# Transposes of the logits ahead of the third stage's first product, in the odd steps of a long convolution with soft mixture of experts

## The chip, the cores and the metric

The program runs on one core of a Trainium2 chip. The metric is the device time of one execution in microseconds (us). Engines: PE (TensorE, with its weight loads as PEld), DVE (VectorE), ACT (ScalarE), POOL (GpSimd) and SP (SyncE, which here only issues transfers). Each engine works through its own instructions in the order of the program and waits on semaphores for the others. All data are float32.

## What is computed

A causal convolution of 8 sequences (5696 tokens, 128 channels) with a filter as long as the sequence, done by Fourier transforms; then a mixture of experts with soft slots over all 45568 tokens. The reference, cut to that:

```python
def _attn_ref(x, h):                       # x (8, 5696, 128), h (5696, 128)
    Xf = np.fft.rfft(x, n=2*S, axis=1)
    Hf = np.fft.rfft(h, n=2*S, axis=0)
    return np.fft.irfft(Xf * Hf[None], n=2*S, axis=1)[:, :S, :]

def _moe_ref(x, phi, w1, w2):              # x (45568, 128), 8 experts of 4 slots
    logits = x @ phi                       # (45568, 32)
    d = softmax(logits, axis=0)            # over the tokens
    slot_input = (d.T @ x).reshape(E, S_per_e, D)
    slot_out[e] = relu(slot_input[e] @ w1[e]) @ w2[e]
    c = softmax(logits, axis=1)            # over the slots
    return c @ slot_out
```

## The kernel before

The transform of a sequence is split into two lengths, 90 and 64, and done as matrix products in three stages. Between stages the data go through HBM, since the next stage needs another axis on the partitions.

- *First stage* (`first_low`, `first_high`, L217): a chunk of the input, `xc`, is folded into sums and differences `x` (`fold`, L207, on POOL once the second stage runs), multiplied by `s1`, copied by ACT from PSUM into `fst` (L220), and stored to `f`.
- *Second stage*: `stage_b1` (L263) multiplies a loaded unit `gt` by `wt` into PSUM `bt`; DVE multiplies that with the filter's spectrum (L281 twice, L290 twice) into `yf`. `stage_b2` (L305) multiplies `yf` by `vt`; ACT copies into `zst` (L311), which is stored to `z`. A step's last unit is left in `wait_b2`, and its L305 is issued in the next step's turn, behind the L263 of the next unit.
- *Third stage*, per pair of chunks T: `load_pair` (L342, five transfers, about 1.3 MB) brings `zc`, of which there is one buffer; `stage_c1` (L361) makes the tokens `y`. It is a generator in three parts: first half (two products `b_`, `a_`; ACT copies `b_` into `y`, L370; DVE adds and subtracts `a_`, L366 and L367), second half (two more products; ACT copies into `om`, L374; the generator yields ahead of the rest), and the rest (`after`: L366 and L367 again, and four operations of POOL, L380).
- *Slots*: `stage_c2` (L391) transposes `y` into `yt`; `stage_c3` (L400) forms the logits, copied by ACT to `lt` (L403); `column_max` (L411 to L419, DVE) keeps the running extreme `low` over tokens. `stage_c4` transposes `lt` on PE (L429, four instructions), copies it to `L` (L433, ACT), writes the exponentials `dt` (L435, ACT, with `low` as bias) and `dn` (L440, ACT), clears a corner of `dt` (L437, POOL), takes a row maximum `rm` of `L` (L444, DVE) and subtracts it (L445, POOL). `stage_c5` (L452) transposes `dt`, `softmax` (L460 to L466) finishes the weights over slots, `dispatch` (L478) sums tokens into slots, `stage_c6` (L504) transposes the weights into `cbatch`.

**Order.** The schedule is manual: every engine works in the order in which the Python code issues. The main loop runs over steps t = 0 to 80. A step processes one chunk of the first stage, one or two units of the second, and half a pair's work of the third; a pair thus takes two steps, a sequence eight (in one step of the eight a unit is half as large). The order within a step is a string, one letter per piece of work: `ORDER_E` for odd t, `ORDER_O` for even t, and the `FILL_` strings for t below 9. In `ORDER_E`:

- `x` loads input, `X` and `Y` are the first stage (products, copies, stores), `f` folds the next input,
- `1`, `j`, `w` take the three parts of `stage_c1` of pair T = (t - 27)/2,
- `4` is `stage_c4` of the pair before (lag of two steps), `b` a turn of the second stage, `5` is `stage_c5`, `s` is `softmax`.

In `ORDER_O`: `z` is `load_pair`, `P` loads units `gt`, `2`, `6`, `d`, `3`, `m` are `stage_c2`, `stage_c6`, `dispatch`, `stage_c3`, `column_max`. The letters `x`, `X`, `Y`, `f` do nothing from t = 72 on, when the first stage has no more chunks, and `4` does nothing before t = 29.

**PSUM.** Four banks turn round for the products of the first and third stage, L305 and all transposes (`bank()`): each request takes the bank of four requests earlier and so waits for whoever read that one. `bt` has two tiles of its own.

After step 80 a hand-written tail with its own order does the last pairs, the experts (L753, L773) and the output (L809 to L820).

Of the kernel before, what the change touches and what calls it, by code (L numbers as in the profile page):

```python
# [77 lines left out]
def kernel(  # L78
# [484 lines left out]
    for comp in range(2):  # L563
        fold(0, comp)
    wait_b2 = []
    ORDER_E, ORDER_O, FILL_E, FILL_O, XAHEAD = "xXYf14jwb5s", "zPxXfb26db3m", "xYfX14jwb5s", "zPxfXb26db3m", 3

    for t in range(last_front + 1):
        us = list(units(t))
# [286 lines left out]
```

## Time and profile before

| | us |
|---|---|
| median of 3 runs | 865.26 |
| lowest, highest | 859.84, 866.72 |
| the profiled execution | 866.74 |
| its span, first to last instruction | 864.4 |

A profile is one execution, recorded instruction by instruction. Its page names an instruction group by line, engine, operation and the tiles it writes and reads (`bank<-zc,i` writes a PSUM bank from `zc` and `i1`). "Idle before" is the time that the engine stood still ahead of an instruction, with the releaser, the event that ended it. Some groups that matter here:

| line, engine | what | count | mean ns of one |
|---|---|---|---|
| L361 PE | products of the third stage, 128x512 | 480 | 618 |
| L429 PE | transposes of `lt`, 128x128 | 128 | 291 |
| L370, L433, L435, L374 ACT | copies and exponential of the third stage | 32 each | 595 to 599 |
| L440 ACT | `dn`, one column | 31 | 189 |
| L366, L367 DVE | sums and differences, 128x512 | 64 each | 689 to 692 |
| L444 DVE | row maximum | 32 | 676 |

Matmuls are pipelined, so the duration of one is longer than its share of PE's time. The granted clock of PE is given as a share of full speed; its mean over the span is 0.947.

### The profile page before, as it was taken

The numbers are of one execution on the slowest core, as the hardware profiler recorded it, in microseconds if no ns is written. First come the engines' busy times: TensorE is split into PE (matmuls) and PEld (weight loads), VectorE is DVE, ScalarE is ACT, GpSimd is POOL, SyncE is SP. The second block draws the span as 40 slices with busy tenths as digits, with TensorE's granted clock in tenths as the row PEclk, the third lists the DMA queues.
The fourth block names the chain that finished last, engine by engine and source line by source line (L and its number), as shares of the span: only waits on it lengthen the run. The fifth ranks groups of instructions, "written<-read, shape, count | busy, mean of one in ns | idle before, by whom it ended". The sixth has DMA issues, their size and how long they took to land.

```text
span 864.4 us, 20502 instructions
## 1 busy us (share of the span) xinstructions
PE 769.7 (89%) x7796; PEld 374.4 (43%) x7796; DVE 626.5 (72%) x942; ACT 437.4 (51%) x967; POOL 374.8 (43%) x359
## 2 busy tenths in 40 slices
PE   5878888779999999999999999999978878978882
PEld 1222333234444444444444444444444444445882
DVE  3259867658777878887888788877778997973542
ACT  3422344435655655665566556656544545562531
POOL 2133424245556556665566555555533443540000
PEclk9999999989999999999999999999999999997755
DMA  9989999999999999999999999999997797760998
GB/s 294 294 268 308 306 319 342 337 335 331 329 323 343 343 349 318 343 337 340 325 336 345 320 339 330 348 312 335 334 333 264 265 316 277 283 276 8 371 380 327
DMA packets 153243, 271.99 MB, mean 315 GB/s; under 512 B 11878, under 2 KB 110054, under 8 KB 150005
## 3 DMA queue, kind: packets, MB, share of 16 engines
q1 hardware_dynamic: 152571, 270.38, 90.5%
q8 instruction: 62, 1.02, 0.4%
q10 hardware_dynamic: 576, 0.31, 0.1%
q14 instruction: 34, 0.28, 0.1%
HBM read 142.57 MB, written 127.98 MB: 313 GB/s over the span
## 4 chain that ended last, share of the span: by engine, by line
PE 58%; DMA 21%; DVE 12%; SPq 3%; issue 2%; ACT 1%; POOL 1%; DVEq 0%; ACTq 0%; POOLq 0%
PE bank L217 14%; PE bank L361 13%; PE bank L305 8%; PE bt L263 7%; PE bank L391 5%; DMA zc<-z 5%; DMA xc<-in_x_dram 5%; DMA out_dram<-o 5%; PE bank L478 3%; DMA gt<-f 3%; DMA xc<-in_h_dram 2%; DVE yf L290 2%; SPq L342 2%; DVE p L281 2%; DVE bt L281 2%
## 5 line engine op out<-in xcount | busy, mean ns | idle before, releaser
L207 POOL TENSOR_TENSOR x<-xc 128x512 f32<-128x512 f32 x126 | 158.0, 1276 | 245.0 <-PE bank L217 177.0
L217 PE MATMUL bank<-x,s 128*64 128x512 f32 (+1 forms) x1152 | 224.6, 610 | 14.0 <-DVE x L207 9.2
L311 ACT ACTIVATE zst<-bank 128x512 f32<-128x512 f32 (+1 forms) x184 | 98.6, 586 | 184.3 <-PE bank L305 165.1
L220 ACT ACTIVATE fst<-bank 128x512 f32<-128x512 f32 x216 | 127.4, 598 | 106.3 <-PE bank L217 87.6
L281 DVE TENSOR_TENSOR p<-bt,Hi 128x1024 f32<-128x1024 f32 x96 | 111.3, 1160 | 32.7 <-PE bt L263 31.6
L361 PE MATMUL bank<-zc,i 128*64 128x512 f32 x480 | 119.1, 618 | 12.4 <-DMA zc<-z 10.0
L305 PE MATMUL bank<-yf,vt 64*64 64x256 f32 x1440 | 100.8, 387 | 25.7 <-DVE yf L290 25.6
L263 PE MATMUL bt<-gt,wt 64*64 64x256 f32 x1620 | 114.3, 389 | 9.6 <-DMA gt<-f 8.1
L290 DVE TENSOR_TENSOR yf<-bt,p 128x512 f32<-128x512 f32 x192 | 119.4, 663 | 3.3
L217 PEld LDWEIGHTS bank<-x,s 128*64 128x64 f32 (+1 forms) x1152 | 55.8, 124 | 150.3 <-issue 79.9
L281 DVE TENSOR_TENSOR bt<-bt,Hr 128x1024 f32<-128x1024 f32 x96 | 113.0, 1177 | 0.0
L263 PEld LDWEIGHTS bt<-gt,wt 64*64 64x64 f32 x1620 | 54.2, 132 | 84.6 <-issue 33.1
L380 POOL TENSOR_TENSOR y<-y,op 128x512 f32<-128x512 f32 x64 | 77.6, 1212 | 13.4 <-DVE op L366 10.4
L305 PEld LDWEIGHTS bank<-yf,vt 64*64 64x64 f32 x1440 | 56.3, 134 | 57.4 <-issue 23.1
L366 DVE TENSOR_TENSOR y<-bank,y 128x512 f32<-128x512 f32 x32 | 22.1, 692 | 77.3 <-PE bank L361 73.8
L380 POOL TENSOR_TENSOR y<-y,om 128x512 f32<-128x512 f32 x54 | 64.1, 1187 | 2.1
L361 PEld LDWEIGHTS bank<-zc,i 128*64 128x64 f32 x480 | 30.9, 139 | 76.8 <-issue 46.6
L391 PE MATMUL bank<-ident,y 109*128 109x109 f32 x512 | 62.4, 272 | 1.3 <-DVE y L380 1.0
L391 PEld LDWEIGHTS bank<-ident,y 109*128 109x128 f32 x512 | 52.1, 147 | 17.2 <-issue 9.2
L393 ACT ACTIVATE yt<-bank 128x360 f32<-128x360 f32 x128 | 51.0, 490 | 2.4 <-PE bank L391 1.8
L809 PE MATMUL op<-so,cT 32*128 32x128 f32 x704 | 45.9, 379 | 5.7 <-ACT o L818 5.2
L466 POOL TENSOR_TENSOR L<-L,rs 128x512 f32<-128x512 f32 x32 | 33.6, 1051 | 31.1 <-DVE rs L465 20.9
(96 smaller groups left out, 792.0 us busy)
## 6 DMA issues: line engine op xcount, KB each, us to landing
gt<-f SPq DMA_DIRECT2D x99, 512.0 KB
z<-zst SPq DMA_DIRECT2D x88, 512.0 KB
f<-fst SPq DMA_DIRECT2D x144, 240.0 KB
zc<-z SPq DMA_DIRECT2D x30, 1024.0 KB
xc<-in_x_dram SPq DMA_DIRECT2D x64, 320.0 KB
f<-fst SPq DMA_DIRECT2D x144, 120.0 KB
out_dram<-o SPq DMA_DIRECT2D x16, 1024.0 KB
zc<-z SPq DMA_DIRECT2D x90, 128.0 KB
```

Source lines behind the costliest of these rows:

```text
L207: eng.tensor_tensor(out=folded(c, comp)[:, :, :], in0=t_[:, 0, :, :], in1=t_[:, 1, ::-1, :], op=AL.subtract if comp else AL.add)
L217: nc.tensor.matmul(p[o * width:(o + 1) * width, :], s1[:, comp + G, k], folded(c, comp)[:, :, :].rearrange("p n d -> p (n d)"), start=True ...
L220: nc.scalar.activation(st[:, :, G, :], p[:, :].rearrange("p (n d) -> p n d", d=D), AF.Copy)
L263: nc.tensor.matmul(bt[q * HP:(q + 1) * HP, a, o, :], wt[r, 2 * i + q, :], t_[r, 2 * o + q, :, :].rearrange("p c d -> p (c d)"), start=True ...
L281: nc.vector.tensor_tensor(out=p_, in0=pv, in1=h_, op=AL.mult)
L290: eng.tensor_tensor(out=y_[r, 0:k, c, :], in0=pv[:, :, c, :], in1=pi[r, 0:k, 1 - c, :], op=op_)
L305: nc.tensor.matmul(bz[q][a * HP:(a + 1) * HP, o * 2 * D:(o + 1) * 2 * D], vt[r, i, a, :], y_[r, a * m + o, :, :].rearrange("p c d -> p (c ...
L311: nc.scalar.activation(st[:, 0:m, q, :], bz[q][:, 0:m * 2 * D].rearrange("p (o x) -> p o x", o=m), AF.Copy)
L361: nc.tensor.matmul(p[h_ * HP:(h_ + 1) * HP, :], i1[0:kr, tab, :], t_[0:kr, h_, o, :, q, :], start=True, stop=True)
L380: eng.tensor_tensor(out=part_, in0=part(v, 0), in1=o_[:, :, :], op=sign)
L391: nc.tensor.transpose(p[:, i * TR:(i + 1) * TR], ys[T][0:TR, k * CH + i, 0:D], ident[0:TR, 0:TR])
L393: nc.scalar.activation(yt[:, k * CH:(k + 1) * CH, :, :], of_tokens(p), AF.Copy)
```

## The change

In the order of odd steps, `4` (`stage_c4`) changes places with `1` (the first part of `stage_c1`). Nothing else is touched; the even steps, the steps below 9 and the tail keep their orders.

```diff
-    ORDER_E, ORDER_O, FILL_E, FILL_O, XAHEAD = "xXYf14jwb5s", "zPxXfb26db3m", "xYfX14jwb5s", "zPxfXb26db3m", 3
+    ORDER_E, ORDER_O, FILL_E, FILL_O, XAHEAD = "xXYf41jwb5s", "zPxXfb26db3m", "xYfX14jwb5s", "zPxfXb26db3m", 3
```

More of the change, by code (lines that the diff above doesn't have):

```diff
@@ L565 @@
     wait_b2 = []
-    ORDER_E, ORDER_O, FILL_E, FILL_O, XAHEAD = "xXYf14jwb5s", "zPxXfb26db3m", "xYfX14jwb5s", "zPxfXb26db3m", 3
+    ORDER_E, ORDER_O, FILL_E, FILL_O, XAHEAD = "xXYf41jwb5s", "zPxXfb26db3m", "xYfX14jwb5s", "zPxXfb26db3m", 3
     for t in range(last_front + 1):
```

## The prediction

> **What bounds the kernel now.** First the page: engines, granted clock and the chain that ended last. (In each fence of a timeline the columns are start, duration, engine, line, operation, out<-in, count, and in brackets the idle time of the engine before it and what ended that.)
>
> ```profile
> PE 769.7 (89%) x7796; PEld 374.4 (43%) x7796; DVE 626.5 (72%) x942; ACT 437.4 (51%) x967; POOL 374.8 (43%) x359
> ...
> PE 58%; DMA 21%; DVE 12%; SPq 3%; issue 2%; ACT 1%; POOL 1%; DVEq 0%; ACTq 0%; POOLq 0%
> ```
>
> PE carries most of the chain, then transfers, then DVE; one stage may be bound by each, so I read the stage that the change touches. The busy times by windows of 20 us give PE 20.00 of 20 in most windows from 200 to 620 us. The exceptions hold a wait of the third stage's first product, found by the timeline of PE alone:
>
> ```profile
> 319.36 1.94 PE L361 MATMUL bank<-zc,i 128*64 128x512 f32 x8 [0.68 <-DMA zc<-z]
> ...
> 400.88 1.94 PE L361 MATMUL bank<-zc,i 128*64 128x512 f32 x8 [0.86 <-ACT fst L220]
> ...
> 482.18 1.94 PE L361 MATMUL bank<-zc,i 128*64 128x512 f32 x8 [0.66 <-DMA zc<-z]
> ...
> 563.83 1.94 PE L361 MATMUL bank<-zc,i 128*64 128x512 f32 x8 [0.58 <-DMA zc<-z]
> ...
> 605.71 1.94 PE L361 MATMUL bank<-zc,i 128*64 128x512 f32 x8 [1.24 <-DMA f<-fst]
> ```
>
> Three more such rows begin at 197.85, 218.21 and 523.12 (0.28, 0.41, 0.35 us), and one at 644.75 (2.61 us). In these PE stands before the product with its input zc late (the two rows that name another releaser I read the same way, as the product waits for all five loads of zc). Then the timeline of all engines over an odd step without such a wait:
>
> ```profile
> 441.39 1.94 PE L361 MATMUL bank<-zc,i 128*64 128x512 f32 x8
> ...
> 441.60 0.60 ACT L220 ACTIVATE fst<-bank 128x512 f32<-128x512 f32 x1 [0.34 <-PE bank L217]
> ...
> 442.51 0.60 ACT L370 ACTIVATE y<-bank 128x512 f32<-128x512 f32 x1 [0.31 <-PE bank L361]
> ...
> 443.44 0.69 DVE L366 TENSOR_TENSOR y<-bank,y 128x512 f32<-128x512 f32 x1 [2.22 <-PE bank L361]
> ...
> 443.95 0.60 ACT L433 ACTIVATE L<-bank 128x512 f32<-128x512 f32 x1 [0.84 <-PE bank L429]
> ...
> 445.90 0.69 DVE L366 TENSOR_TENSOR op<-bank,om 128x512 f32<-128x512 f32 x1 [0.45 <-PE bank L361]
> ...
> 451.06 1.09 PE L305 MATMUL bank<-yf,vt 64*64 64x256 f32 x16
> ```
>
> PE runs without a gap, and ACT and DVE stand waiting for it. Last, an odd step after the first stage has ended (no L217 between L400 and L361):
>
> ```profile
> 664.30 1.94 PE L361 MATMUL bank<-zc,i 128*64 128x512 f32 x8
> 664.63 0.49 ACT L403 ACTIVATE lt<-bank 128x360 f32<-128x360 f32 x1
> ...
> 667.76 0.61 ACT L435 ACTIVATE dt<-lt,low 128x360 f32<-128x360 f32 x1 [0.30 <-DVE low L416]
> 667.78 0.69 DVE L366 TENSOR_TENSOR y<-bank,y 128x512 f32<-128x512 f32 x1
> ...
> 669.71 0.68 DVE L366 TENSOR_TENSOR op<-bank,om 128x512 f32<-128x512 f32 x1
> ...
> 674.86 1.09 PE L305 MATMUL bank<-yf,vt 64*64 64x256 f32 x16 [2.67 <-DVE yf L290]
> ```
>
> Here DVE has no gap from 662.83 until yf, and PE waits 2.67 us for it: this stretch is DVE's.
>
> **What the change moves.** Nothing is added or removed. In 26 odd steps (t = 29 to 79) stage_c4 is issued before the first half of stage_c1. On PE four transposes go ahead of four products; on ACT the copy of L, the two exponentials (dt, dn) go ahead of the copy of y (L370); on DVE the reduction rm (L444) goes ahead of the first pair L366/L367. The orders of POOL and SP are the same instruction for instruction, so no load or store is issued in another order. I take three kinds of step.
>
> **An ordinary step (21 or so of 26): nothing.** The chain gives 0.59 us of PE time for four transposes and 1.87 for four products. From 441.39 on: transposes to 441.98, eight products to 445.72, now 443.84 + 1.87 = 445.71: the same end. ACT is free at 442.20 (441.60 + 0.60). L starts there; today dt follows L by 0.49, dn follows dt by 0.50, the next copy follows dn by 0.09 (starts 443.95, 444.44, 444.94, 445.03), so y starts at 443.28 and ends at 443.88 instead of 443.11. The product for the first pair ends at 441.98 + 1.87 = 443.85. The pair starts near 443.97, 0.53 later than today, and ends at 443.97 + 0.73 + 0.69 = 445.39. The second pair waits for the last product and starts at 445.90 as today. So the reordering of ACT and DVE hides in 0.5 us of DVE's waiting; whatever exceeds that goes straight to yf (L290), whose reader L305 has nothing to spare: yf ends at 449.62 + 1.29 = 450.91, and L305 (451.06) follows the end of yf by the 0.14 that the chain shows elsewhere. The rest has more room: lt, which the transposes read, was copied 2.9 us before (458.26 + 0.49 = 458.75 in the next such step, product at 461.65); the work that covers this is the first stage's 3.72 us of products. The bank rotation shifts: the last product now takes the transposes' bank, free at 442.80, needed at 444.8; the second L305 bank waits for the first pair, done 445.39, needed near 447. POOL gets rm earlier, and frees its queue at most 0.3 us sooner (446.60 for 446.89), for which PE doesn't wait.
>
> **Steps in which zc is late: a gain.** The transposes don't need zc, so they run in the wait. Each gains the smaller of the wait and 0.59: 0.59 at 319.36, 400.88, 482.18, 0.58 at 563.83 (2.35 in all), and 0.28, 0.41, 0.35, 0.59 (1.63) at 197.85, 218.21, 523.12, 605.71. At most 4.0. The other end is 0: if transfers alone set when zc lands, PE gets to the next late step sooner and waits longer there. The share of DMA in the window of 20 us that follows decides: it is 0.94, 0.92, 0.92, 0.93 after the first four and 0.96 to 0.99 after the others, so after the first four transfers themselves stand idle for over a microsecond of those 20, and an earlier PE lets them start earlier. I take the first four whole and half of the other four: 2.35 + 0.8 = 3.1.
>
> SP's rows of issuing (merged, with short waits in them) fill 16.9 us of the period of 20.26 from 441.39 to 461.65. The Trainium skill ("Perfetto Trace Analysis", What "DMA-bound" means) calls a kernel bound by its DMA sequencer where that track is solid slices, time of descriptors and not of data; by that rule zc would land no sooner, this term would be 0 and the sum +0.6. The track has gaps here, so I keep the windows.
>
> **The step at 644.75: a gain.** PE waits from 642.1; lt is copied at 642.41 + 0.48 = 642.89, so the transposes fit ahead of zc. At a lowered clock they took 1.05 us of the chain there: that is the lower end, 1.1. The upper end takes the slow products back as well: the eight cost 2.76 and 2.24 where 1.94 and 1.94 is usual, so 1.1 + 0.8 + 0.3 = 2.2. What slowed them is the wait of 2.61 us, after which the granted clock of the window 640 to 660 is 0.83; transposes in the middle cut it into pieces of about 1 us. I take 1.5, nearer to the lower, as only part of the slowing need go.
>
> The Trainium skill ("TensorE: Matmul & The Clock Gate", What's actually happening) has the clock fall after an idle window of some 3.4 us; by that, a wait of 2.61 would not lower it and 1.1 would be the gain, the sum -2.1. The row says that 2.61 was enough.
>
> **Three steps without first-stage work (664.30, 683.16, 701.91): a loss.** The cover is gone. lt ends at 664.63 + 0.49 = 665.12, so the transposes, due at 664.30, start near 665.25 (0.14 after it, as L429 follows L370 at 443.25): PE stalls 0.95, ends the last product at 665.25 + 0.59 + 3.74 = 669.58 for 668.62. Behind the transposes in PE's queue stand the products, behind the exponential in ACT's the copy of y. The exponential waits for low (L416), which DVE delivers at 667.67 whatever happens, so dt starts at 667.76 as now, dn at 668.27, y at 668.36, ending 668.96. DVE fills 0.67 of its wait with rm, then starts the first pair at 669.0, ends it at 670.4, and only then the second: 0.7 after today's 669.71. The products (669.58) are no later than that. yf and L305 are 0.7 late: 3 x 0.7 = 2.1. Ends: 0 if DVE makes it up, 2.9 if the whole 0.95 stall of PE comes through.
>
> **Sum.** -3.1 - 1.5 + 2.1 = -2.5 us. The profiled execution took 866.74 (span 864.4 and 2.3 around it), 1.5 above the median 865.26 of the runs shown; against it 864.2, against the median 862.8.
>
> **The rivals.**
> - *Handed back.* Transfers set the pace; the 3.1 is gone, leaving -1.5 + 2.1 = +0.6: 865.9. For it: DMA shares of 0.97 to 1.00. Against: the idle transfers after late steps.
> - *Slower: ACT's queue holds back the first pair.* Place: copy of y behind two exponentials, in the 22 steps t = 29 to 71. It decides from the point at which the first pair starts more than 0.5 us later than I worked out (ACT late with the first stage's copies, or the exponential waiting for low there too). Every 0.1 beyond costs 22 x 0.1 = 2.2. At 0.4 beyond: 8.8 + 2.1 - 1.5 = +9.4, 874.7. Against: low is ready at 440.87 + 0.16 = 441.03, 1.7 us before dt would need it (442.69).
> - *Faster by more.* The waits vanish altogether, 5.06 in the eight and 2.61, with the slow clock's 1.1, and DVE absorbs the loss: -8.8, 856.5. Against: the transposes hold only 0.59 of a wait.
> - That the change doesn't do what it says is out: the transposes do move on PE.
>
> **Chances.** Forecast 0.66, handed back 0.17, slower rival 0.10 (0.09 of it beyond 1%), faster rival 0.07. One per cent, 8.7 us, is about what a measurement of this kernel can tell from no change. So faster 0.07, within 0.84, slower 0.09. Range: the terms' ends give -4.0 - 2.2 + 0 = -6.2 (859.1) and 0 - 1.1 + 2.9 = +1.8 (867.1); the runs shown spread from 859.84 to 866.72, so I widen both by nearly 2: 857.5 to 869.
>
> **What will show it.** Right: L361 directly after L217 gone, L429 there with no idle before it; waits of L361 on zc shorter by up to 0.59, the one at 644.75 by a microsecond; second L366 unchanged against the last product in ordinary steps; L429 idle about 0.95 before itself in three late steps, waiting for ACT lt L403, and L305's wait for yf. Wrong: idle of L305 on yf in ordinary steps (slower rival), or late steps whose zc wait is as long as before (handed back). A median outside 857.5 to 869 makes the whole wrong.

## The result, and the profile after

The changed kernel takes 866.61 us (median of 20 runs, 860.38 to 873.36), the one before 865.84 (20 runs, 859.7 to 872.31). The ratio is 1.0009, 95% interval 0.9987 to 1.0031: no difference that these runs can tell, and at most 0.13% gained. Two of the changed kernel's runs (873.36 and 873.3) count as slow and stand outside the ratio; without them its median is 865.92. The profiled execution of the changed kernel has a span of 865.2 us, against 864.4.

The page of the changed kernel, engines and chain:

```profile
PE 770.4 (89%) x7796; PEld 379.3 (44%) x7796; DVE 627.4 (73%) x942; ACT 435.6 (50%) x967; POOL 374.7 (43%) x359
...
PE 58%; DMA 19%; DVE 14%; SPq 3%; issue 3%; ACT 2%; POOL 1%; DVEq 0%; ACTq 0%; POOLq 0%
```

Almost nothing moves on the page. That is not because nothing happened. The timeline of all engines over an ordinary odd step of the changed kernel:

```profile
443.23 0.66 PE L429 MATMUL bank<-ident,lt 128*128 128x128 f32 x4
443.82 3.65 PE L361 MATMUL bank<-zc,i 128*64 128x512 f32 x16
...
445.00 0.59 ACT L370 ACTIVATE y<-bank 128x512 f32<-128x512 f32 x1
445.87 0.69 DVE L366 TENSOR_TENSOR y<-bank,y 128x512 f32<-128x512 f32 x1 [0.56 <-PE bank L361]
...
447.59 0.69 DVE L366 TENSOR_TENSOR op<-bank,om 128x512 f32<-128x512 f32 x1 [0.30 <-PE bank L361]
...
452.75 1.09 PE L305 MATMUL bank<-yf,vt 64*64 64x256 f32 x16
```

The transposes stand first and wait for nothing. The second pair of DVE starts 4.36 us after the step's first PE instruction; before it was 445.90 - 441.39 = 4.51. From one such step to the next the changed kernel takes 20.10 us (423.13, 443.23), the old one 20.26 (421.13, 441.39). The timeline of PE alone, changed kernel, at the products that wait:

```profile
299.78 3.65 PE L361 MATMUL bank<-zc,i 128*64 128x512 f32 x16 [0.99 <-DMA zc<-z]
...
318.85 0.66 PE L429 MATMUL bank<-ident,lt 128*128 128x128 f32 x4
322.07 5.23 PE L361 MATMUL bank<-zc,i 128*64 128x512 f32 x16 [2.56 <-DMA zc<-z]
...
485.02 3.65 PE L361 MATMUL bank<-zc,i 128*64 128x512 f32 x16 [1.16 <-ACT dt L435]
...
567.03 5.35 PE L361 MATMUL bank<-zc,i 128*64 128x512 f32 x16 [1.97 <-DMA zc<-z]
```

These waits come on top of the 0.59 us that the transposes now cover (a row that names another releaser is read as in the prediction: a late zc). In this execution there are fewer of them than in the one before, but they are longer, and after two of them the products run slowly: 5.23 and 5.35 us instead of 3.65, at a granted clock of 0.73 from 322 to 328 us and 0.72 from 567 to 573. Here is where the time of single executions went, in two stretches, from the timelines of PE: from the start of step t = 29 (197.57 before, 197.49 after) to that of t = 71, and from there to the first product of the tail that follows an L400 (both in us).

| kernel, profiled execution | two ordinary steps | waits of L361, first stretch | first stretch | second stretch |
|---|---|---|---|---|
| before | 20.26 | 5.06 | 428.40 | 108.44 |
| changed | 20.10 | 7.64 | 430.95 | 105.81 |

In the first stretch the change saves 21 x 0.16 = 3.4 us, and pays 2.6 in longer waits and (5.23 - 3.65) + (5.35 - 3.65) = 3.3 in slow products: +2.5, the difference of the stretches. The whole of the two spans adds up as -0.1 up to t = 29, +2.5, -2.6, and +1.0 in the tail, whose order is the same in both: +0.8. These are two single executions; how much of it belongs to the order is for the experiments.

### The profile page after: what moved, and what is told of

Same layout as the page of the kernel before. It is cut to its first block, busy times and chain, and to the rows that moved or that the text cites. A ratio compares the mean times of both kernels' runs of the same rounds, so it can differ in the third digit from the quotient of the medians.

```text
span 865.2 us, 20505 instructions
## 1 busy us (share of the span) xinstructions
PE 770.4 (89%) x7796; PEld 379.3 (44%) x7796; DVE 627.4 (73%) x942; ACT 435.6 (50%) x967; POOL 374.7 (43%) x359
## 4 chain that ended last, share of the span: by engine, by line
PE 58%; DMA 19%; DVE 14%; SPq 3%; issue 3%; ACT 2%; POOL 1%; DVEq 0%; ACTq 0%; POOLq 0%
PE bank L217 16%; PE bank L361 11%; PE bank L305 8%; PE bt L263 7%; PE bank L391 6%; DMA out_dram<-o 5%; DMA zc<-z 4%; DMA xc<-in_x_dram 4%; PE bank L478 3%; DMA gt<-f 3%; DVE yf L290 3%; DVE p L281 2%; DVE bt L281 2%; PE bank L400 2%; DMA xc<-in_h_dram 2%
## 5 line engine op out<-in xcount | busy, mean ns | idle before, releaser
L217 PE MATMUL bank<-x,s 128*64 128x512 f32 (+1 forms) x1152 | 228.3, 615 | 12.2 <-DVE x L207 8.4
L220 ACT ACTIVATE fst<-bank 128x512 f32<-128x512 f32 x216 | 127.5, 598 | 105.3 <-PE bank L217 71.8
L361 PE MATMUL bank<-zc,i 128*64 128x512 f32 x480 | 115.9, 625 | 13.5 <-DMA zc<-z 11.4
L217 PEld LDWEIGHTS bank<-x,s 128*64 128x64 f32 (+1 forms) x1152 | 56.6, 125 | 151.8 <-issue 80.6
L305 PE MATMUL bank<-yf,vt 64*64 64x256 f32 x1440 | 100.1, 383 | 24.4 <-DVE yf L290 24.4
L305 PEld LDWEIGHTS bank<-yf,vt 64*64 64x64 f32 x1440 | 56.0, 133 | 55.7 <-issue 16.5
L361 PEld LDWEIGHTS bank<-zc,i 128*64 128x64 f32 x480 | 35.2, 142 | 73.2 <-issue 55.9
L391 PE MATMUL bank<-ident,y 109*128 109x109 f32 x512 | 64.0, 276 | 1.3 <-DVE y L380 1.0
L391 PEld LDWEIGHTS bank<-ident,y 109*128 109x128 f32 x512 | 53.4, 149 | 16.6 <-issue 10.4
L444 DVE TENSOR_REDUCE rm<-L 128x16 f32<-128x512 f32 x32 | 21.9, 684 | 40.8 <-POOL x L207 37.5
```

The lines of the kernel that those rows point to most:

```text
L217: nc.tensor.matmul(p[o * width:(o + 1) * width, :], s1[:, comp + G, k], folded(c, comp)[:, :, :].rearrange("p n d -> p (n d)"), start=True ...
L220: nc.scalar.activation(st[:, :, G, :], p[:, :].rearrange("p (n d) -> p n d", d=D), AF.Copy)
L305: nc.tensor.matmul(bz[q][a * HP:(a + 1) * HP, o * 2 * D:(o + 1) * 2 * D], vt[r, i, a, :], y_[r, a * m + o, :, :].rearrange("p c d -> p (c ...
L361: nc.tensor.matmul(p[h_ * HP:(h_ + 1) * HP, :], i1[0:kr, tab, :], t_[0:kr, h_, o, :, q, :], start=True, stop=True)
L391: nc.tensor.transpose(p[:, i * TR:(i + 1) * TR], ys[T][0:TR, k * CH + i, 0:D], ident[0:TR, 0:TR])
```

## The experiments

**Is it the transfers?** In both orders the loads of the input were left out from the second sequence on, some 11% of what a step transfers (the output is then not the convolution of that input).

```diff
         g, j = divmod(c, NJ)
+        if g > 1:
+            xs[c] = xcs[c % len(xcs)]
+            return
```

With the old order:

> The old order, with the loads of the input left out from the second sequence on (the folds read what the buffers hold), so with some 11% less to transfer per step of the main stretch. Theory A (transfers set the pace, and what the new order saves on PE comes back as waiting for zc): between 200 and 620 us no wait of L361 for zc is left, and two ordinary steps take 20.26 us of PE as before. Theory B (the waits for zc come from the order of the engines and not from transfers): waits for zc of 0.3 to 1.2 us stay, one or two to a sequence.

With the new order:

> The new order with the same loads left out. Theory A: no waits for zc either, two ordinary steps take 20.10 us (the eight products of the third stage run in one go, 3.58 instead of 1.87 + 1.87), so PE reaches t = 72 about 21 x 0.16 = 3.4 us sooner than in light_before, counted from t = 29; whole kernel 1 to 3.5 us faster than light_before. Theory C (the 0.16 is chance of one execution): 20.26 in both, and no difference up to t = 72.

Measured: 849.53 us (4 runs, ratio to before 0.9821, 0.9774 to 0.9868) with the old order, 846.67 (4 runs, 0.9802, 0.9753 to 0.9851) with the new. The intervals overlap, so the steps must decide. Busy times by windows of 100 us: first the stretch of time, then PE, PEld, DVE, ACT and POOL, then granted clock, share of DMA, GB/s. Before:

```profile
500.00:600.00 100.00, 98.72 (x1028) 46.31 (x1028) 79.62 (x124) 59.36 (x136) 59.46 (x55) 1.00 0.98 335
```

The new order with the loads left out:

```profile
500.00:600.00 100.00, 99.65 (x1037) 47.00 (x1036) 81.93 (x126) 60.25 (x141) 59.43 (x56) 1.00 0.89 306
```

DMA falls from 0.98 to 0.89 busy and PE has no gap left but the 0.35 us of the short step. Between 200 and 600 us neither light kernel has a wait for zc. Two ordinary steps take 20.26 with the old order and 20.10 to 20.11 with the new, every time; the first stretch is 422.96 and 419.63, 3.3 us apart as worked out. In the chain that ended last, in order of time, the old kernel shows (start, us, what)

```profile
421.20 1.87 PE bank L361 x8
423.07 0.59 PE bank L429 x4
423.66 1.87 PE bank L361 x8
```

and light_after (its line numbers are 3 higher)

```profile
408.04 0.59 PE bank L432 x4
408.62 3.58 PE bank L364 x16
```

So theory A holds and B and C fall: the order does save PE time, 0.16 us a pair, as the eight products take 3.58 us in one go and 3.74 in two halves. With the full transfers this time doesn't reach the end, as the next runs show.

**Which steps matter?** Each order in one part only.

```diff
-        for c_ in ((ORDER_E if full else FILL_E) if t % 2 else (ORDER_O if full else FILL_O)):
+        for c_ in (((ORDER_E if t < NA else "xXYf14jwb5s") if full else FILL_E) if t % 2 else (ORDER_O if full else FILL_O)):
```

> The new order up to t = 71, the old one in the four odd steps without first-stage work. Theory A: within 2 us of before and of the new order; up to t = 72 no sooner than before, as the waits for zc grow by what is saved; no stall of L429 on lt after 640 us. Theory D (the gain in ordinary steps is real and is lost again in the four last steps): about 3 us faster than before.

And the reverse (old order, with "xXYf41jwb5s" from t = 73 on):

> The old order up to t = 71, the new one in the four odd steps without first-stage work. Theory A and the prediction's step: L429 waits 0.80 us for lt in each of the four; from the third of them on each step is 0.3 to 0.7 us longer than before; the whole within 2 us of before. Theory D: 2 to 3 us slower than before.

Measured: 867.89 us (1.001, 0.9981 to 1.0038) and 865.09 (1.0002, 0.9975 to 1.0029): neither differs from before, and theory D falls: 3 us faster (0.9965) lies outside the first interval; in the second 2.5 us slower is just inside, but there the stretch after t = 71 is 4 us shorter and not longer. The stretches of all six kernels:

| kernel | order, first stretch | first stretch | waits of L361 in it | order, second | second stretch |
|---|---|---|---|---|---|
| before | old | 428.40 | 5.06 | old | 108.44 |
| split14_41 | old | 432.25 | 8.94 | new | 104.46 |
| changed | new | 430.95 | 7.64 | new | 105.81 |
| split41_14 | new | 430.38 | 9.98 | old | 108.06 |
| light_before | old | 422.96 | 0 | old | 104.94 |
| light_after | new | 419.63 | 0 | new | 104.44 |

With full transfers the first stretch is the same for both orders within the spread of two executions each (428 to 432); only with lighter ones is the new order ahead. The old order alone ranges from 5.06 to 8.94 in its waits, so the pair before and changed doesn't show by itself that the waits grew with the order. Two executions each: the old order waits 7.0 us on average, the new one 8.8, and 10.5 with half of the 3.3 of slow products in the changed kernel. That is 3.5 more, and 3.4 is what it saves; with a spread of 4 us this agrees with theory A but doesn't measure it. The second stretch is 0.5 to 4 us shorter with the new order, which the prediction had as a small loss. The medians don't show that gain: 4 us in an otherwise equal execution would be a ratio of 0.9954, and the interval of split14_41 begins at 0.9975. How far the shorter second stretch holds in other executions stays open.

Of what was expected, L429 stands 0.80 to 0.81 us before itself for lt in each of split14_41's last four odd steps, and not once in split41_14's. The steps of split14_41 are not each 0.3 to 0.7 us longer: the last two take 18.02 and 19.54 us, against 18.75 and 19.27 in before.

**What makes zc late once in eight steps?** The store of the slot weights, `c_t`, goes out one pair ahead of those loads. It was left out for five of six sequences (the tail then reads the first one's weights again in their place).

```diff
-        if not tail and last_of == NQ - 1:
+        if not tail and last_of == NQ - 1 and b == 0:
...
-                                  in_=cd[b].rearrange("p r j -> p (r j)"))
+                                  in_=cd[0].rearrange("p r j -> p (r j)"))
```

> The old order; the store of the slot weights (c_t, 712 KB, once in eight steps) is left out for five of six sequences, and their loads at the end read the first one again. Theory A (transfers set the pace; that store, issued one pair ahead, is what makes zc late once in eight steps): the waits of L361 for zc in the last pair of a sequence (0.86, 0.66, 0.58, 2.61 us before) shrink to under 0.3, ordinary steps stay at 20.26, about 4 to 6 us faster than before. Theory E (that store has nothing to do with it): the waits stay.

> The new order with the same stores left out. Theory A: the waits for zc are shorter than those of the new order (0.15 to 2.56 us), ordinary steps 20.10, and the kernel is up to 3 us faster than noct_before, as there is now something to spare on the transfers. Theory E: waits of 1 to 2.5 us as in the new order, no faster than noct_before.

Measured: 860.48 us (10 runs, 0.9942, 0.9911 to 0.9973) with the old order, 858.06 (10 runs, 0.9921, 0.9895 to 0.9947) with the new. From the second sequence on (after 390 us) neither profile holds a wait for zc, and ordinary steps take 20.26 and 20.10; the first stretch takes 427.75 and 423.78. Theory A again; E falls. The store is not the only cause, though: ahead of 390 us both profiles still wait 4.7 and 3.9 us for zc, and the longest wait of noct_before, 2.16 us at 281.50, ends before the first such store is issued (302.77). The 2.4 us between the two medians have the sign of the 3.4 saved in ordinary steps. The two intervals, each against before, overlap; set against each other, the ten runs each differ by 2.2 us in the mean, with a 95% interval of 0.2 to 4.2. So here some of the saving reaches the end.

**Does one go save it also the other way, and has yf slack?** The transposes behind both halves, with light transfers.

```diff
-    ORDER_E, ORDER_O, FILL_E, FILL_O, XAHEAD = "xXYf14jwb5s", "zPxXfb26db3m", "xYfX14jwb5s", "zPxfXb26db3m", 3
+    ORDER_E, ORDER_O, FILL_E, FILL_O, XAHEAD = "xXYf1j4wb5s", "zPxXfb26db3m", "xYfX14jwb5s", "zPxfXb26db3m", 3
```

> With the loads of the input left out as in light_before: the transposes behind both halves of the third stage's products instead of between or ahead of them. If running the eight products in one go is what saves 0.16 us, they take 3.58 here too. On DVE rm then comes between the two pairs, waits for the copy of L, and puts the second pair about 1.8 us later; if yf has no slack against L305, that lateness appears as a wait of L305 for yf in every ordinary step, and two steps take 21.5 to 22 us. If there is slack, 20.1.

The timeline of all engines over one odd step of that kernel (line numbers 3 higher):

```profile
427.02 3.65 PE L364 MATMUL bank<-zc,i 128*64 128x512 f32 x16
...
430.61 0.66 PE L432 MATMUL bank<-ident,lt 128*128 128x128 f32 x4
...
432.00 0.69 DVE L447 TENSOR_REDUCE rm<-L 128x16 f32<-128x512 f32 x1 [1.50 <-ACT L L436]
432.60 0.68 DVE L369 TENSOR_TENSOR op<-bank,om 128x512 f32<-128x512 f32 x1
...
437.75 1.09 PE L308 MATMUL bank<-yf,vt 64*64 64x256 f32 x16 [0.72 <-DVE yf L293]
```

One execution: 882.5 us. The products again take 430.61 - 427.02 = 3.59 in one go. The second pair starts 5.58 us after the step's first PE instruction instead of 4.36, L308 (old L305) waits 0.72 for yf, L220 (old L217) another 0.32 for a bank that the second pair holds, and two steps take 21.32. The lateness is 1.2 us rather than the 1.8 expected, and it all reaches PE: yf has no slack, as the prediction said.

**Could the wait be covered whole?** The second stage's turn was put ahead too.

```diff
-    ORDER_E, ORDER_O, FILL_E, FILL_O, XAHEAD = "xXYf14jwb5s", "zPxXfb26db3m", "xYfX14jwb5s", "zPxfXb26db3m", 3
+    ORDER_E, ORDER_O, FILL_E, FILL_O, XAHEAD = "xXYfb41jw5s", "zPxXfb26db3m", "xYfX14jwb5s", "zPxfXb26db3m", 3
```

> A whole kernel: the turn of the second stage goes ahead too (order b41jw5s), so that 0.59 + 1.9 us of PE work that doesn't need zc stands before the third stage's product. Theory A: waits for zc of up to 2.5 us are covered, L429 waits no more for lt in the last odd steps, and L305's waits for yf (0.35, 2.5) go; what is left is set by transfers, at a DMA share of 0.98 to 1.00: 4 to 10 us faster than before. Rival F (the tokens y come 1.9 us later, POOL's four operations on them then end behind their transposes in the next step): L391 waits 1 to 2 us for POOL in each even step, 10 us or more slower.

Measured: 875.68 us (6 runs, 1.0136, 1.0094 to 1.0178). The waits by pairs on PE from 200 to 620 us, with total, times and longest:

```profile
PE bank L391 <- ACT yt L393: 7.0, 13, 0.5
PE bank L391 <- POOL y L380: 5.3, 12, 0.7
PE bt L263 <- DMA gt<-f: 0.2, 1, 0.2
```

Not one wait for zc or yf is left there, as theory A said, but F's mechanism has come: the tokens come later, and their transposes wait. The rows name yt for some, but in the timeline the fourth group of transposes starts at 458.12, just behind POOL's last operation on y (455.61 + 2.46 = 458.07). It is 0.5 us a pair, less than F's 1 to 2, but it comes in every pair, and ordinary steps take 20.62 us. Up to t = 71 this costs no more than the waits for zc that it replaces: that stretch takes 430.74, against 430.95 in the changed kernel. The kernel is slower behind it: there it takes 115.76 us against 105.81, 10 of the 12.4 us between the two spans (877.6 and 865.2), and L391 waits 13.3 us for POOL's y, against 0.3. In the last four even steps, which have no first-stage products, these waits are 2.7 to 3.5 us a step, more than F's 1 to 2.

**Could a load make room?** After the store `c_t` the next load of input was issued behind the loads of zc, nothing left out; in both orders.

```diff
+        def late_x(t):
+            if t >= NA:
+                return []
+            if t % NJ == NJ - 1 and LAG_C < t < NA - NJ:
+                return []
+            first = t - 1 if t % NJ == 0 and LAG_C < t - 1 < NA - NJ else t
+            return range(first + XAHEAD, t + XAHEAD + 1)
...
-            "x": lambda: load_x(t + XAHEAD) if t < NA else None,
+            "x": lambda: [load_x(c) for c in late_x(t)],
```

> A whole kernel: the new order, and in the odd step after the store of the slot weights (c_t) the load of the next input chunk (356 KB) is issued behind the next loads of zc instead of ahead of them; nothing is left out. Theory A with noct's finding (that store, 712 KB ahead of zc, is what makes zc late): 356 KB of the queue's work is moved behind zc, about 1.1 us at 330 GB/s; the waits for zc in the last pair of a sequence, about 0.6 to 2.6 us behind the transposes, shrink by about 1 us each, 3 to 6 us faster than before. If transfers as a whole set the pace (nothing is saved by order), the waits appear in the pairs after it, and the time is within 2 us of before.

> The same deferral with the old order. If it removes the waits: 1 to 4 us faster than before, and 1 to 3 us slower than defer_after, whose ordinary steps are 0.16 us shorter. If transfers as a whole set the pace: as defer_after, within 2 us of before.

Measured: 873.15 us both times (7 runs each; 1.0105, 1.0069 to 1.0142 with the new order, 1.0087, 1.0048 to 1.0126 with the old). That is slower than either expectation. The timeline of all engines in defer_after, in a step that uses the deferred load:

```profile
410.64 2.49 POOL L207 TENSOR_TENSOR x<-xc 128x512 f32<-128x512 f32 x2 [11.58 <-DMA xc<-in_x_dram]
413.19 0.11 POOL L437 MEMSET dt<- 64x8 f32 x1
...
413.35 0.66 PE L452 MATMUL bank<-ident,dt 128*128 128x128 f32 x4 [3.08 <-POOL dt L437]
```

The wait for zc is all but gone (one of 0.6 us from 200 to 620) and a longer one has come: the load itself is now late, POOL's fold waits for it, and behind the fold in POOL's queue stands the memset of `dt`, for which PE waits. Five such waits make 11.9 us from 200 to 640 (8.8 in defer_before). A late transfer pushed aside makes the next one late. The profiled executions, 868.28 and 867.42, are each the shortest of their seven, 5 to 6 us under the median; they show the mechanism, not where the rest of the loss went. No version that was run beats both kernels with its work complete.

## Why the prediction held, and what in it did not

The range and "within 1%" held. The likeliest course did not: -2.5 us is a ratio of 0.9971, below the interval. What came is nearest to the rival called *handed back*: the time saved ahead of t = 71 is waited away again. That its sum, +0.6, lies so near the 0.77 between the medians is luck: it has -1.5 + 2.1 for the last steps, where the profiled pair has -2.6, and the profiled pair comes to +0.8 only by +2.5 ahead of them and +1.0 in the tail, which no term foresaw.

- *Ordinary steps: nothing.* Wrong by a small amount, in every step. The prediction added 0.59 + 1.87 + 1.87 on either side and got the same end. The 1.87 was read where the transposes stand between the halves; eight products in one go take 3.58 (light_after, light_1j4). The profile of before had this already, in its tail, where no transposes stand between (timeline of PE):

```profile
739.32 3.65 PE L361 MATMUL bank<-zc,i 128*64 128x512 f32 x16
742.90 1.72 PE L391 MATMUL bank<-ident,y 109*128 109x109 f32 x16
```

  742.90 - 739.32 = 3.58. (Of the 26 steps 14 are ordinary, not 21 or so, beside the eight late ones, the one at 644.75 and the three last; the 0.16 comes in the late ones too.) The cover that it named for ACT and DVE held: the second pair still starts 0.19 us behind the last product. The first pair starts 0.59 later in the step (445.87 - 443.23 = 2.64 against 443.44 - 441.39 = 2.05), where 0.53 was worked out, and the spare time took it up.
- *Late zc: -3.1.* This term failed. It took idle transfers in the window after a late step (0.92 to 0.94) for time that an earlier PE could fill. The waits did not shrink by what the transposes cover: they are 7.64 and 9.98 us in the two executions with the new order there, 5.06 and 8.94 with the old, and in the changed kernel's the clock took 3.3 more. The light pair shows that the transfers set this, since the same order with 11% less to transfer keeps its gain; noct shows one transfer that tips it over. Why just these executions had one wait of 2.56 and one of 1.97 is a matter of single executions: split41_14, the same order there, has eleven of 0.21 to 1.64 instead.
- *The step at 644.75: -1.5.* Right in sign, too small: from that step's start to the next one's the old order took 22.16 us (23.01 in split41_14), the new one 18.39 (18.18 in split14_41), some 4 us less. In light_before and light_after, with a shorter wait there, it is 19.76 and 18.66. In the noct pair no zc is late there, and the new order is 0.65 longer (16.54 and 17.19): the gain hangs on the late load. The transposes cut the wait:

```profile
646.70 0.66 PE L429 MATMUL bank<-ident,lt 128*128 128x128 f32 x4 [0.81 <-ACT lt L403]
...
648.47 3.65 PE L361 MATMUL bank<-zc,i 128*64 128x512 f32 x16 [1.11 <-DMA zc<-z]
```

  (timeline of PE, changed kernel): 0.81 and 1.11 instead of 2.61 in one, and the products at 3.65 where they had taken 2.76 and 2.24. The upper end, full clock at once, was the right one, and it went on past the products (L305 there 1.09 for 1.98).
- *Three late steps: +2.1.* The mechanism is there, row by row, a little smaller; in this pair the clock hides it. Timeline of all engines, changed kernel:

```profile
684.54 0.66 PE L429 MATMUL bank<-ident,lt 128*128 128x128 f32 x4 [0.80 <-ACT lt L403]
...
687.13 0.60 ACT L435 ACTIVATE dt<-lt,low 128x360 f32<-128x360 f32 x1 [1.30 <-DVE low L416]
...
687.73 0.57 ACT L370 ACTIVATE y<-bank 128x512 f32<-128x512 f32 x1
...
688.33 0.69 DVE L366 TENSOR_TENSOR y<-bank,y 128x512 f32<-128x512 f32 x1 [0.50 <-ACT y L370]
...
689.66 0.68 DVE L366 TENSOR_TENSOR op<-bank,om 128x512 f32<-128x512 f32 x1
...
694.81 1.09 PE L305 MATMUL bank<-yf,vt 64*64 64x256 f32 x16 [2.54 <-DVE yf L290]
```

  The exponential waits for low, y behind it, the first pair 0.50 for y; L305 starts 11.07 us after the step's start (683.74) instead of 10.56 (693.72 - 683.16): 0.5 late, not 0.7. But the step is 18.01 us long, not 18.75 + 0.5: this time PE came out of its wait at full clock (1.09, where the old kernel's L305 took 1.98). All three steps take 57.08 us (664.28 to 721.36) against 56.88. The other profiles show the size. With the new order the three take 57.0 to 57.1 in all five that have it there, at a mean granted clock of 0.94. With the old order they take 55.6 in three, also at 0.94 (split41_14, light_before, defer_before), 56.88 at 0.91 in before and 58.05 at 0.88 in noct_before. So at the same clock the loss is 1.5, three times the 0.5, and a lower clock in the old order's executions can hide it.
- *The slower rival* (ACT's queue holding back DVE in ordinary steps) fell: L305's waits for yf from 160 to 640 us are 6.4 us in both.
- Of the two rules of the Trainium skill, "Perfetto Trace Analysis" (What "DMA-bound" means) pointed the right way for the zc term, 0 in place of -3.1; how near its sum of +0.6 came is the luck named above. The runs do not show that it is the issuing track rather than the transfers behind it that binds: leaving transfers out relieves both. "TensorE: Matmul & The Clock Gate" (What's actually happening) gave a step at 644.75 worth 1.1, and the row was nearer: the clock fell after waits well under 3.4 us. The same section has the window run freely, so that equal waits can fare differently; this would leave a fall after a wait shorter than the window unexplained, and no run here shows the window.

Left open: why two halves cost 0.16 us more than one go, whether the late transfers are bound at SP's issuing or at the engines behind it, and why the shorter second stretch of the profiles doesn't show in the medians.

## What to carry to other kernels

When PE and the transfers are both near their limit (here PE gap-free and DMA 0.97 busy), time saved on PE can come back as a longer wait for a later load; test this by leaving out some transfers in both versions before believing a gain or its absence. Covering or moving one late transfer is not enough: moved work meets the next in-order queue, as the fold and the memset behind it did. One profile of each kernel is one execution of each: here two executions of one order differ by 4 us in the stretch that the change was to shorten by 3.4. An idle share after a stall is no proof that the resource has time to spare.

## What the runs showed that was not expected

Eight products of 128x512 run in 3.58 us in one go and in 3.74 with four transposes between their halves, in every ordinary step of the profiles read for it. The granted clock fell after waits of 1.97 and 2.56 us (products 5.35 and 5.23 instead of 3.65) but not after those of 2.20 and 2.36 in split14_41 (clock 1.00, products 1.94 and 1.94) nor one of 2.50 in defer_before (products 1.94), so the length of a wait alone does not tell whether the clock falls.
